# A linear attention and two MLPs on one core: the second pair of token chunks gets block products in its second layer, and work beside it goes to other steps

## The chip, the cores and the metric

The kernel runs on one core of one Trainium2 chip. The metric is the device time of one execution in microseconds, as the median of several runs. TensorE multiplies, VectorE (DVE in the profile) and ScalarE (ACT) convert, add and evict, GpSimd (POOL) and SyncE (SP) mostly issue DMAs. The clock that TensorE is granted has two levels, 1.2 and 2.4 GHz, and the profile gives it as a share of full speed.

## The reference

```python
# attention: q is normalised over the head's columns, k over the sequence
kv = np.einsum('bhsd,bhse->bhde', k_s, v)
x = np.einsum('bhsd,bhde->bhse', q_s, kv)      # 8 x 8 x 576 x 64 -> 4608 tokens x 512
# first MLP: 512 -> 2048 -> 512
h = x @ w_in
x = np.maximum(0.01 * h, h) @ w_out
# second MLP (MLP2): 512 -> 3 x 768 -> 512
h = np.maximum(np.maximum(x @ w1, x @ w2), x @ w3)
out = h @ w_out
```

Everything must come out with the accuracy of float32. The inputs come as 64-bit words; the kernel converts the weights itself.

## The kernel before

**Tiling.** The 4608 tokens are nine chunks of 512. Each operand of a matmul is split into a high and a low half in fp32r, and a product is three matmuls (high x high, high x low, low x high) of 128 x 128 by 128 x 512.

**First stage.** Chunks 0 to 2 go through the first MLP one by one (lines 1139 to 1196), m = 0 to 15 over blocks of 128 hidden columns, while attention for the next chunks and the conversion of the weights run beside them.

**Pairs.** Chunks 3 to 8 go through it as three pairs, `APAIRS` (line 30). Two chunks side by side are a 2 x 2 block matrix, and the first layer multiplies it by seven block products instead of eight (Strassen's scheme in Winograd's form, names a11, a12, s2, s1, s3, a22, s4). `InnerUnit` t = 0 to 7 does two m each: 7 products of 6 matmuls. The second layer of the first two pairs is plain: `out_a` (line 1210) multiplies the split halves of g (`split_g`, line 819) by weights `outw`, over 16 m for the left side beside the first layer and 16 m for the right side behind it; each side has 4 x 16 x 3 = 192 matmuls. The third pair goes through `inner_and_outer` (line 1758): its first layer writes quarters of the hidden matrix (`OuterPair.quarter`), and its second layer is seven block products behind it, 28 `TERMS` (name, q) of 12 matmuls. `build` makes the split operands `opO` three terms ahead, `load` fetches the weights `sumw` (each serves two terms), `finish` and `send` add and store the results. From term 18 `operands` builds what MLP2 needs first.

**MLP2** then takes five `PAIRS` in units u = 0 to 8 of seven block products, and for the first four pairs a `last_layer` (line 1516) of 21 terms with weights `lastw`. The first-MLP results of chunks 0 and 1 are partial sums in DRAM. `join` (line 938) adds them with accumulating DMAs on POOL's queue; `JOIN_AT` says in which pair's last layer.

**Order.** Work beside the main line is a set of generators: `background(step)` starts those whose step has come and advances each by one `yield`. Steps 0 to 47 are the first stage, 48 to 79, 80 to 111 and 112 to 143 the three pairs, in a plain pair three for each t and then one for every two m. `plan_units` gives attention its steps, `ahead_units` (line 948) the rest: `stage_a` and `sums_a` (sums of first-layer weights), `sums_out` (sums of second-layer weights, into `stream_sums`), `ahead_unit` (conversion, sums and split of MLP2's weights, into `stream`) and `ahead_out` (into `stream_last`). A planner orders what is ready on each engine; `pin` keeps an instruction in program order. So DMAs that depend on nothing late can run well ahead of their step.

**Room.** The pool `wp` has 17 buffers of 8 KB a partition, tag `w`, shared by weights, operands, quarters and rooms of the work beside; `xp` has two each of `xhi` and `xlo`, for attention results (`side`) and the rooms of the first weight units; `gp` has g, ghi, glo and st. PSUM has four banks `acc` and four `ps`.

Of the kernel before, what the change touches and what calls it, by code (L numbers as in the profile page):

```python
# [18 lines left out]
P = 128  # L19
N = 512  # L20
# [64 lines left out]
def tile_kernel(ctx: ExitStack, tc: tile.TileContext, q, k, v, wa, wb, out):  # L85
# [70 lines left out]
    newest = {}  # L156
    posted = []
# [87 lines left out]
    def to_stream(u, t, part):  # L245

        i = place(part, u)
        pin(nc.gpsimd.dma_start(stream[:, i], t))
        if i < 3:
            pin(nc.gpsimd.dma_start(stream[:, CYCLE + i], t))  # L250

# [94 lines left out]
    def ahead_out(t):  # L346
# [28 lines left out]
        for i, z in enumerate((more, room)):  # L375
            z = z.rearrange("p (h b n) -> p b h n", h=2, n=H)
            for b in range(4):
                pin(nc.gpsimd.dma_start(stream_last[:, 4 * i + b, t], z[:, b]))

    wos = {}  # L380

    def load_wo(t):

        w = wos[t] = wp.tile([P, 2, 2, N], F32R, tag="w", name="wo")
        for i, part in enumerate(("a11", "a12", "a21", "a22")):
            m, f = i % 2, i // 2
            to = w[:, :, m, f * H : f * H + H]
            pin(nc.sync.dma_start(to.bitcast(F32), stream_last[:, PARTS.index(part), t]))
# [471 lines left out]
    def stage_a(m):  # L860

        w = tiles[m].bitcast(F32)
        nc.sync.dma_start(stream_out[:, m], w[:, :, 1])
        i = m // 2 * len(AUSES)
        quarters = w[:, :, 0].rearrange("p h (b n) -> p b h n", n=H)
        for b in range(2):
            if m % 2 == 0:
                nc.sync.dma_start(stream_in[:, i + AUSES.index(("a11", "a12")[b])], quarters[:, b])
            elif b == 1:
                nc.sync.dma_start(stream_in[:, i + AUSES.index("a22")], quarters[:, b])  # L870
        yield

    def sums_a(t):
# [13 lines left out]
        for h, z in enumerate((hi, lo)):  # L887
            for at, n in ((0, 1), (1, 1), (2, 2)):
                to = i + AUSES.index(PARTS[4 + at])
                nc.sync.dma_start(stream_in[:, to : to + n, h], z[:, at : at + n])  # L890

    def sums_out(t):
# [12 lines left out]
        for h, z in enumerate((hi, lo)):  # L905
            nc.sync.dma_start(stream_sums[:, :, t // 4, h, t % 4], z)

# [7 lines left out]
    def plan_units(c):  # L915

        early = c < EARLY
        for hp in range(NP):
# [19 lines left out]
    def join(c):  # L938
# [169 lines left out]
    def load_in(g):  # L1108

        w = wp.tile([P, 4, 2, H], F32R, tag="w", name="group")  # L1110
        at = 4 * g % (len(AUSES) * MB_OUT)
        tc.keep_in_program_order(nc.sync.dma_start(w.bitcast(F32), stream_in[:, at : at + 4]))
# [7 lines left out]
    def load_out(n):  # L1120

        w = wp.tile([P, 2, 2, N], F32R, tag="w", name="outw")
        t = n % MB_OUT
        tc.keep_in_program_order(nc.sync.dma_start(w.bitcast(F32), stream_out[:, 2 * t : 2 * t + 2]))
        outs[n] = w

    def out_w(n):
# [3 lines left out]
        while len(outs) <= min(ahead, 2 * MB_OUT * (len(APAIRS) - 1) - 1):  # L1131
# [127 lines left out]
    def load_group(g):  # L1259
# [12 lines left out]
        for a, e in runs:  # L1272
            if a < e:
                ins = nc.sync.dma_start(w[:, a:e].bitcast(F32), stream[:, at + a : at + e])
# [46 lines left out]
    class Unit:  # L1321
# [14 lines left out]
        def snap(self, bank):  # L1336
            t = bp[0].tile([P, N], F32, tag="snap", name="snap", bufs=5)[:, : self.n]
            nc.scalar.activation(t, bank[:, : self.n], AF.Copy)  # L1338
            return t

        def out(self, i, bank, snap=None):

            bank = bank[:, : self.n]
            if self.j == 0:
                if self.layer is not None:
                    g = self.layer.quarter(i % 2 * 2 + i // 2, self.t)
                else:
                    tag, bufs = (("g", 2), ("ghi", 2), ("glo", 2), ("st", 4))[i]
                    g = gp.tile([P, N], F32, tag=tag, name=f"best{i}", bufs=bufs)[:, : self.n]
# [49 lines left out]
    class LastLayer:  # L1399
# [14 lines left out]
        def build(self, upto):  # L1414

            while len(self.made) < min(upto, len(LAST_TERMS)):
# [8 lines left out]
                tags = (("ghi", "glo"), ("ghi", "glo"), ("g", "g"), ("st", "st"), ("st", "st"))[k % 5]  # L1425
                hi, lo = (
                    gp.tile([P, N], F32R, tag=tag, name="opL", bufs=4 if tag == "st" else 2) for tag in tags
                )
# [6 lines left out]
        def load(self, upto):  # L1435

            while len(self.loaded) < min(upto, len(OUT_ORDER)):
# [3 lines left out]
                else:  # L1441
                    w = wp.tile([P, 4, 2, H], F32R, tag="w", name="lastw")[:, : MB // 2]
                pin(nc.sync.dma_start(w.bitcast(F32), stream_last[:, PARTS.index(name)]))
# [207 lines left out]
    class OuterPair:  # L1651
# [8 lines left out]
        def pair_of(self, x, q):  # L1660

            key = (x % 2, q)
            if key not in self.rooms:
                if q < 2 and x % 2 == 0:
# [28 lines left out]
        def load(self, upto):  # L1693

            for k in range(len(self.loaded), min(upto, 2 * len(OUT_ORDER))):
# [3 lines left out]
                if name in OUT_SUMS:  # L1699
                    pin(nc.sync.dma_start(f, stream_sums[:, OUT_SUMS.index(name), half]))  # L1700
                else:
                    odd, right = {"a11": (0, 0), "a12": (1, 0), "a22": (1, 1)}[name]
                    z = slice(MA // 2 * half + odd, MA // 2 * (half + 1), 2)
                    for h in range(2):
# [53 lines left out]
    def inner_and_outer(i, ops, fills):  # L1758
# [16 lines left out]
        for k, (name, q) in enumerate(TERMS):  # L1775
# [24 lines left out]
            if k == 18:  # L1800
                building = operands(quarters_b(sides), nxt, operand, fixed=True) if last else a_operands(i + 1, nxt)
            if k >= 18:
# [14 lines left out]
    for i in range(len(APAIRS)):  # L1817
        ops, nxt, building = begun_a, {}, iter(())
        last = i == len(APAIRS) - 1
        if last:  # L1820
# [8 lines left out]
            break  # L1829
# [59 lines left out]
        fills = [lambda f=f, i=i, pairs=pairs: out_a(i, 1, MA // 2 - 1, f, pairs) for f in range(KDM)]  # L1889
    for p in range(len(PAIRS)):  # L1890
# [3 lines left out]
        for u in range(NU):  # L1894
# [7 lines left out]
            iteration(Unit(p, u, ops, best, layer), *fill)  # L1902
            if not last and u in (3, 6):
# [89 lines left out]
```

## Time and profile before

| | us |
|---|---|
| median of 3 runs (lowest to highest) | 1378.44 (1372.72 to 1379.41) |
| profiled execution, own time | 1376.07 |
| its span, first to last instruction | 1374.3 |
| TensorE busy | 1347.8 |
| VectorE busy | 1007.1 |
| ScalarE busy | 710.9 |

The granted clock is full in all 40 slices of the page. Durations of matmuls overlap, so a rate is read from how long a run of them took. In the stages named below, the second pair's first layer begins at 473 us, interleaved with the end of the first pair, its second layer goes on until 693.7, the third pair's second layer runs from 761.9 to 848.4, and MLP2 follows.

### The profile page before, as it was taken

Reading aid. Unit: us, or ns where it says so; the run is one execution under the profiler, and the core shown is the slowest. Engines: PE = TensorE matmul, PEld = TensorE weight load, DVE = VectorE, ACT = ScalarE, POOL = GpSimd, SP = SyncE. Lnnn points to the kernel's source line nnn. Section 1 sums busy time; section 2 is a strip of 40 time slices with the busy share of each in tenths; the row PEclk is TensorE's granted clock in tenths of the full one; section 3 lists DMA queues with packets and bytes.
Section 4 is the critical chain, followed back from the end, with each engine's and each line's share of the span. In section 5 each row is a group of like instructions: output and inputs, shape, how many; then the busy total and the mean of one; then the engine's idle time right before and its main releaser. Section 6 shows DMA issues by size and latency. Waiting matters only on the chain.

```text
span 1374.3 us, 18904 instructions
## 1 busy us (share of the span) xinstructions
PE 1347.8 (98%) x6638; PEld 1107.5 (81%) x6638; DVE 1007.1 (73%) x1747; ACT 710.9 (52%) x1452; POOL 164.6 (12%) x251
## 2 busy tenths in 40 slices
PE   6999999999999999999999999999999999999998
PEld 5788877888788788888788888887788888888897
DVE  9988968864887797855958889767558657755743
ACT  6755857753776665744556554334225324423422
POOL 2001202200112120210313121211000000000000
PEclk9999999999999999999999999999999999999999
DMA  8698865535999967979678898999875584676684
GB/s 313 247 320 318 321 245 171 185 109 222 354 336 358 395 238 281 356 252 384 238 271 292 317 340 313 421 303 309 282 284 170 168 360 142 207 279 221 209 262 174
DMA packets 129502, 376.81 MB, mean 274 GB/s; under 512 B 12800, under 2 KB 68352, under 8 KB 105600
## 3 DMA queue, kind: packets, MB, share of 16 engines
q1 hardware_dynamic: 109936, 304.56, 61.1%
q0 software_dynamic: 18752, 66.72, 14.9%
q10 hardware_dynamic: 720, 4.33, 0.8%
q8 instruction: 53, 0.87, 0.2%
q14 instruction: 41, 0.34, 0.1%
HBM read 285.90 MB, written 96.99 MB: 279 GB/s over the span
## 4 chain that ended last, share of the span: by engine, by line
PE 89%; DVE 4%; DMA 3%; ACT 2%; issue 1%; SPq 0%; DVEq 0%; ACTq 0%
PE ps L1099 44%; PE acc L802 21%; PE ps L802 9%; PE acc L1456 6%; PE acc L1721 5%; PE ps L1456 1%; PE ps L628 1%; PE ps L496 1%; DMA lastw<-stream_last 1%; DMA outw<-stream_out 1%; PE ps L1721 1%; DMA spare<-in_q_dram 1%; DMA sumw<-stream_out 1%; DVE glo L826 0%; DVE opA L1060 0%
## 5 line engine op out<-in xcount | busy, mean ns | idle before, releaser
L1099 PE MATMUL ps<-op,group 128*128 128x512 f32 (+1 forms) x1890 | 395.7, 368 | 3.2 <-ACT snap L1338 3.2
L1099 PEld LDWEIGHTS ps<-op,group 128*128 128x128 f32 x1890 | 331.0, 188 | 65.5 <-ACT snap L1338 5.6
L1099 PE MATMUL ps<-opA,group 128*128 128x512 f32 x1008 | 241.5, 391 | 0.0
L1099 PEld LDWEIGHTS ps<-opA,group 128*128 128x128 f32 x1008 | 188.4, 188 | 39.8 <-ACT snap L1231 0.4
L1338 ACT ACTIVATE snap<-ps 128x512 f32<-128x512 f32 (+1 forms) x135 | 70.5, 552 | 196.4 <-PE ps L1099 191.8
L802 PE MATMUL acc<-ghi,outw 128*128 128x512 f32 x512 | 165.9, 392 | 1.5 <-ACT ghi L825 1.1
L802 PE MATMUL acc<-ghi,w 128*128 128x512 f32 x384 | 128.0, 394 | 1.7 <-ACT ghi L825 1.7
L802 PE MATMUL ps<-xhi,w 128*128 128x512 f32 x384 | 126.4, 393 | 1.1 <-ACT g L1151 0.7
L802 PEld LDWEIGHTS acc<-ghi,outw 128*128 128x128 f32 x512 | 95.4, 188 | 22.6 <-ACT ghi L825 2.5
L1358 DVE TENSOR_TENSOR snap<-snap,ps 128x512 f32<-128x512 f32 (+1 forms) x90 | 56.6, 632 | 77.5 <-ACT snap L1338 66.4
L1456 PE MATMUL acc<-opL,lastw 128*128 128x512 f32 x432 | 102.6, 394 | 1.8 <-DMA lastw<-stream_last 1.8
L802 PE MATMUL acc<-glo,outw 128*128 128x512 f32 x256 | 100.4, 393 | 1.3 <-DVE glo L826 1.1
L1456 PEld LDWEIGHTS acc<-opL,lastw 128*128 128x128 f32 x432 | 81.9, 190 | 19.9 <-ACT snap L1338 2.2
L1429 ACT ACTIVATE opL<-room 128x512 fp32r<-128x512 f32 x84 | 51.8, 629 | 73.6 <-DVE room L1360 38.4
L802 PEld LDWEIGHTS acc<-ghi,w 128*128 128x128 f32 x384 | 71.9, 188 | 18.0 <-ACT ghi L825 2.3
L802 PEld LDWEIGHTS ps<-xhi,w 128*128 128x128 f32 x384 | 72.0, 188 | 17.7 <-ACT g L1151 1.1
L826 DVE TENSOR_TENSOR glo<-g,ghi 128x512 fp32r<-128x512 f32 x80 | 54.8, 687 | 40.4 <-ACT ghi L825 40.2
L802 PE MATMUL acc<-glo,w 128*128 128x512 f32 x192 | 75.4, 393 | 0.0
L802 PE MATMUL ps<-xlo,w 128*128 128x512 f32 x192 | 74.9, 390 | 0.0
L1430 DVE TENSOR_TENSOR opL<-room,opL 128x512 fp32r<-128x512 f32 x84 | 56.6, 683 | 17.4 <-ACT opL L1429 16.6
L1721 PE MATMUL acc<-opO,sumw 128*128 128x512 f32 x288 | 66.6, 389 | 0.7 <-DMA sumw<-stream_out 0.7
L1721 PEld LDWEIGHTS acc<-opO,sumw 128*128 128x128 f32 x288 | 54.0, 188 | 12.3 <-DMA sumw<-stream_out 1.1
(220 smaller groups left out, 2094.5 us busy)
## 6 DMA issues: line engine op xcount, KB each, us to landing
group<-stream SPq DMA_DIRECT2D x78, 1024.0 KB, 9.0
group<-stream_in SPq DMA_DIRECT2D x42, 1024.0 KB, 7.3
outw<-stream_out SPq DMA_DIRECT2D x32, 1024.0 KB, 8.8
lastw<-stream_last SPq DMA_DIRECT2D x28, 768.0 KB, 4.7
stream<-room POOLq DMA_DIRECT2D x66, 256.0 KB, 4.1
raw<-in_wa_dram SPq DMA_DIRECT2D x16, 1024.0 KB, 7.1
room<-in_wb_dram POOLq DMA_DIRECT2D x24, 512.0 KB, 7.5
x<-st SPq DMA_DIRECT2D x40, 256.0 KB, 3.1
```

What stands on the lines that cost most here:

```text
L496: ins = nc.tensor.matmul(acc[z, : D + 1], lhsT=ke[:, r, z], rhs=vt[:, r, h], start=r == 0, stop=r == RK - 1)
L628: nc.tensor.matmul(both(xps, c0, c1), lhsT=a, rhs=halves(y, c0, c1), start=i == 0, stop=i == 2)
L802: ins = nc.tensor.matmul(acc, lhsT=l, rhs=r, start=first and i == 0, stop=last and i == 2)
L826: nc.vector.tensor_tensor(lo[:, z], g[:, z], hi[:, z].bitcast(F32), op=ALU.subtract)
L1099: ins = nc.tensor.matmul(bank[:, : r.shape[1]], lhsT=l, rhs=r, start=fresh and first, stop=last, skip_group_check=not fresh)
L1338: nc.scalar.activation(t, bank[:, : self.n], AF.Copy)
L1358: nc.vector.tensor_tensor(snap, snap, bank, op=ALU.add)
L1429: nc.scalar.activation(hi, z, AF.Copy)
L1430: nc.vector.tensor_tensor(lo, z, hi.bitcast(F32), op=ALU.subtract)
L1456: nc.tensor.matmul(banks[f], lhsT=l, rhs=r, start=fresh and first, stop=final, skip_group_check=not fresh)
L1721: nc.tensor.matmul(banks[f], lhsT=l, rhs=r, start=fresh and first, stop=final, skip_group_check=not fresh)
```

## The change

The second pair goes through `inner_and_outer` too (`PLAIN_OUT = 1` says how many pairs stay plain). Its quarters lie in buffers `w`, and those of x even and q = 3 in two buffers of a new tile `both` in `gp`, which holds ghi and glo side by side. The operands for the next pair are begun at term `NEXT_AT` = 20 in a pair that isn't the last. The steps of `sums_out` (`SO`), `ahead_unit` (`UA`), `ahead_out` (`AO`), `sums_a` (`SA`) and of attention (`LATER`) become tables with other numbers, and a weight unit is done in one go (`alone`) from u = 6 on, formerly from step 101 on. The joins are advanced at named units of MLP2, and before each adding DMA an ACT copy out of the newest `snap` and a small DMA of that copy stand in POOL's queue. Asserts (`need`) tell that what a load reads was written earlier in the program.

```diff
+NEXT_AT = 20
+PLAIN_OUT = 1
+SO = (45, 49, 51, 67, 68, 80, 81, 83)
+UA = (71, 77, 88, 98, 102, 106, 111, 114, 114)
+AO = (126, 131, 144)
+SA = (32, 34, 39, 44, 48, 53, 56, 60)
+LATER = ((0, 0), (43, 2.5), (71, 2.5))
+ALONE = 6
-JOIN_AT = (2, 1)
+JOIN_AT = ((2, 1), (2, 3), (2, 5), (2, 7), (1, 1), (1, 3), (1, 5))
...
-        hi = gp.tile([P, N], F32R, tag="ghi", name="ghi")
-        lo = gp.tile([P, N], F32R, tag="glo", name="glo")
+        both = gp.tile([P, 2, N], F32R, tag="both", name="ghl")
+        hi, lo = both[:, 0], both[:, 1]
...
-                start, lag = CONV * MA + 2 * MA * (i - 1) - (0, 3, 8)[i] + 2.5 * (4 * at + hp), 3
+                start, lag = LATER[i][0] + LATER[i][1] * (4 * at + hp), 3
...
-        for turn in mine[1:]:
+        for i, turn in enumerate(mine[1:]):
+            at = 4 * c + i
+            nc.scalar.activation(column[:, 0, at : at + 1], newest["snap"][:, 0:1], AF.Copy)
+            pin(nc.gpsimd.dma_start(column[:, 1, at : at + 1], column[:, 0, at : at + 1]))
             for z in (slice(0, 2), slice(2, 4)):
                 pin(nc.gpsimd.dma_start(joined[c][:, z], x2[turn][:, z], accum_op=ALU.add))
             yield
-            yield
...
-            yield (29, 34, 39, 44, 48, 52, 56, 60)[t], sums_a(t)
-        for t, at in enumerate((49, 50, 51, 73, 81, 82, 83, 84)):
-        for u, at in enumerate((68, 78, 88, 98, 103, 107, 112, 115, 119)):
-            yield at, ahead_unit(u, at > 100)
-        for t, at in enumerate((127, 135, 143)):
+            yield SA[t], sums_a(t)
+        for t, at in enumerate(SO):
+        for u, at in enumerate(UA):
+            yield at, ahead_unit(u, u >= ALONE)
+        for t, at in enumerate(AO):
...
-        live.extend(join(n) for n, p in enumerate(JOIN_AT) if p == layer.p)
...
         def pair_of(self, x, q):
             key = (x % 2, q)
+            if self.i < len(APAIRS) - 1 and key == (0, MA // 4 - 1):
+                if (x, q) not in self.rooms:
+                    self.rooms[x, q] = gp.tile([P, 2, N], F32, tag="both", name="quarter")
+                return self.rooms[x, q]
...
-            if k == 18:
+            if k == (18 if last else NEXT_AT):
                 building = operands(quarters_b(sides), nxt, operand, fixed=True) if last else a_operands(i + 1, nxt)
...
-            (ops, fills) = inner_and_outer(i, ops, fills)
+        if i >= PLAIN_OUT:
+            begun_a, fills = inner_and_outer(i, ops, fills)
+            ops = begun_a
...
+    joins = join(1), join(0)
...
+            if (p, u) in JOIN_AT:
+                next(joins[JOIN_AT.index((p, u)) < 4], None)
```

## Rows read from the trace of the kernel before

**Rows 1.** The page: busy us (share) x instructions; chain's shares by engine.
```profile
PE 1347.8 (98%) x6638; PEld 1107.5 (81%) x6638; DVE 1007.1 (73%) x1747; ACT 710.9 (52%) x1452; POOL 164.6 (12%) x251
PE 89%; DVE 4%; DMA 3%; ACT 2%; issue 1%; SPq 0%; DVEq 0%; ACTq 0%
```

**Rows 2.** Timeline of TensorE: start, length, line, tiles, shape, how many in a row.
```profile
345.05 4.24 PE L1099 MATMUL ps<-opA,group 128*128 128x512 f32 x18
...
776.50 11.04 PE L1721 MATMUL ps<-opO,sumw 128*128 128x512 f32 x48
```

**Rows 3.** Instructions of line 802: count, ns min/median/max, first and last start.
```profile
L802 PE MATMUL acc<-ghi,outw x512: 387/389/504, 339.3 to 693.7; 128*128 128x512 f32 x171
...
L802 PE MATMUL acc<-glo,outw x256: 387/389/505, 339.5 to 693.5; 128*128 128x512 f32 x128
```

**Rows 4.** Waits of TensorE, 530 to 694: us in total, times, longest.
```profile
PE acc L802 <- DVE glo L826: 1.1, 2, 0.6
PE acc L802 <- ACT ghi L825: 0.5, 1, 0.5
```

**Rows 5.** Waits of TensorE in the third pair, 694 to 850.
```profile
PE acc L1721 <- DMA sumw<-stream_out: 0.7, 1, 0.7
```

**Rows 6.** Timeline of TensorE in MLP2's first last layer.
```profile
960.34 5.96 PE L1456 MATMUL acc<-opL,lastw 128*128 128x512 f32 x18 [1.82 <-DMA lastw<-stream_last]
```

**Rows 7.** The stretch behind that wait: busy by engine, clock, DMA share, GB/s.
```profile
960.30:963.90 3.60, 3.56 (x9) 2.83 (x10) 0.17 (x1) 0.00 (x0) 0.00 (x0) 0.53 1.07 330
```

**Rows 8.** DMA, 925 to 962: POOL's queue (packets, MB, share); issues, us to landing.
```profile
q0 software_dynamic: 1004, 3.65, 51.8%
...
x<-x POOLq DMA_DIRECT2D x6, 512.0 KB, 9.5
lastw<-stream_last SPq DMA_DIRECT2D x3, 768.0 KB, 15.7
```

**Rows 9.** Stages: us, then busy PE, PEld, DVE, ACT, POOL; clock, DMA share, GB/s.
```profile
530.30:693.70 163.40, 161.56 (x728) 132.06 (x727) 117.75 (x198) 93.92 (x187) 31.89 (x45) 1.00 0.81 298
693.70:761.90 68.20, 68.20 (x302) 56.50 (x301) 45.72 (x68) 39.76 (x68) 19.17 (x28) 1.00 0.83 304
761.90:848.40 86.50, 85.81 (x379) 70.75 (x378) 80.43 (x97) 47.87 (x65) 11.70 (x18) 1.00 0.90 333
...
1081.00:1156.00 75.00, 74.31 (x328) 61.22 (x327) 42.89 (x66) 21.06 (x38) 0.00 (x0) 1.00 0.77 266
```

**Rows 10.** VectorE by line, 512 to 694 and 770 to 850: count | busy us, mean ns.
```profile
L826 DVE TENSOR_TENSOR glo<-right,ghi 128x512 fp32r<-128x512 f32 x19 | 12.9, 684 | 7.0 <-ACT ghi L825 6.9
...
L295 DVE TENSOR_TENSOR room<-room 128x512 fp32r<-128x512 f32 x15 | 9.9, 682 | 2.6 <-ACT room L294 2.6
L1060 DVE TENSOR_TENSOR opA<-side,opA 128x1024 fp32r<-128x1024 f32 x7 | 8.4, 1220 | 0.3 <-ACT opA L1059 0.3
L320 DVE TENSOR_TENSOR room<-room 128x1024 f32<-128x1024 f32 x5 | 6.1, 1221 | 0.1
...
L255 DVE TENSOR_TENSOR room<-room 128x256 f32<-128x256 f32 x9 | 3.8, 417 | 0.0
...
L281 DVE TENSOR_SCALAR room<-room 128x1024 f32<-128x1024 f32 x4 | 2.8, 688 | 1.1 <-ACT room L280 1.1
...
L1687 DVE TENSOR_TENSOR opO<-quarter,opO 128x1024 fp32r<-128x1024 f32 x25 | 30.3, 1220 | 4.5 <-ACT opO L1686 4.2 <-DMA group<-stream 0.3
```

**Rows 11.** Timeline of ScalarE: the first eviction of chunk 7's attention.
```profile
519.47 0.60 ACT L772 ACTIVATE side<-ps 128x512 f32<-128x512 f32 x1 [3.90 <-DMA stream<-room]
```

**Rows 12.** Timeline of TensorE: the second pair's second unit begins.
```profile
519.09 0.96 PE L1099 MATMUL ps<-opA,group 128*128 128x512 f32 x3
```

**Rows 13.** SyncE's own waits, 500 to 600: us in total, times, longest.
```profile
SPq L906 <- ACT hi L263: 14.4, 2, 10.4
```

**Rows 14.** The page's 40 slices of 34 us: VectorE's busy tenths.
```profile
DVE  9988968864887797855958889767558657755743
```

**Rows 15.** DMA issues, 765 to 850: KB each, us to landing.
```profile
sumw<-stream_sums SPq DMA_DIRECT2D x8, 1024.0 KB, 7.1
```

More of the change, by code (lines that the diff above doesn't have):

```diff
@@ L156, in tile_kernel, with need @@
     newest = {}
+    written = set()
+    def need(*keys):
+        assert written.issuperset(keys), [key for key in keys if key not in written]
     posted = []
@@ L378, in ahead_out @@
                 pin(nc.gpsimd.dma_start(stream_last[:, 4 * i + b, t], z[:, b]))
+                written.add(("last", 4 * i + b, t))
     wos = {}
@@ L387, in load_wo @@
             to = w[:, :, m, f * H : f * H + H]
+            need(("last", PARTS.index(part), t))
             pin(nc.sync.dma_start(to.bitcast(F32), stream_last[:, PARTS.index(part), t]))
@@ L863, in stage_a @@
         nc.sync.dma_start(stream_out[:, m], w[:, :, 1])
+        written.add(("out", m))
         i = m // 2 * len(AUSES)
@@ L868, in stage_a @@
                 nc.sync.dma_start(stream_in[:, i + AUSES.index(("a11", "a12")[b])], quarters[:, b])
+                written.add(("in", i + AUSES.index(("a11", "a12")[b])))
             elif b == 1:
                 nc.sync.dma_start(stream_in[:, i + AUSES.index("a22")], quarters[:, b])
+                written.add(("in", i + AUSES.index("a22")))
         yield
@@ L890, in sums_a @@
                 nc.sync.dma_start(stream_in[:, to : to + n, h], z[:, at : at + n])
+                written.update(("in", to + k) for k in range(n) if h == 1)
     def sums_out(t):
@@ L906, in sums_out @@
             nc.sync.dma_start(stream_sums[:, :, t // 4, h, t % 4], z)
+        written.add(("sums", t))
     def load_a(m):
@@ L1111, in load_in @@
         at = 4 * g % (len(AUSES) * MB_OUT)
+        need(*(("in", at + k) for k in range(4)))
         tc.keep_in_program_order(nc.sync.dma_start(w.bitcast(F32), stream_in[:, at : at + 4]))
@@ L1123, in load_out @@
         t = n % MB_OUT
+        need(("out", 2 * t), ("out", 2 * t + 1))
         tc.keep_in_program_order(nc.sync.dma_start(w.bitcast(F32), stream_out[:, 2 * t : 2 * t + 2]))
@@ L1130, in out_w @@
             ahead = max(ahead, min(n + AHEAD_OUT, n // (2 * MB_OUT) * 2 * MB_OUT + 2 * MB_OUT + 1))
-        while len(outs) <= min(ahead, 2 * MB_OUT * (len(APAIRS) - 1) - 1):
+        while len(outs) <= min(ahead, 2 * MB_OUT * PLAIN_OUT - 1):
             load_out(len(outs))
@@ L1273, in load_group @@
             if a < e:
+                need(*(("b", at + k) for k in range(a, e)))
                 ins = nc.sync.dma_start(w[:, a:e].bitcast(F32), stream[:, at + a : at + e])
@@ L1338, in snap @@
             nc.scalar.activation(t, bank[:, : self.n], AF.Copy)
+            newest["snap"] = t
             return t
@@ L1347, in out @@
                 else:
-                    tag, bufs = (("g", 2), ("ghi", 2), ("glo", 2), ("st", 4))[i]
-                    g = gp.tile([P, N], F32, tag=tag, name=f"best{i}", bufs=bufs)[:, : self.n]
+                    if i == 2:
+                        t = gp.tile([P, 2, N], F32, tag="both", name="best12")[:, :, : self.n]
+                        self.best[1], self.best[2] = t[:, 0], t[:, 1]
+                    elif i != 1:
+                        tag, bufs = (("g", 2), None, None, ("st", 4))[i]
+                        self.best[i] = gp.tile([P, N], F32, tag=tag, name=f"best{i}", bufs=bufs)[:, : self.n]
+                    g = self.best[i]
                 self.best[i] = g
@@ L1424, in build @@
                 z = {"a11": b11, "a12": b21, "s2": b11, "s3": b12, "s1": b12, "a22": b21, "s4": b22}[name]
[L1425 to L1428, printed above, removed]
+                tag = ("both", "both", "g", "st", "st")[k % 5]
+                if tag == "both":
+                    o = gp.tile([P, 2, N], F32R, tag=tag, name="opL")
+                    hi, lo = o[:, 0], o[:, 1]
+                else:
+                    hi, lo = (
+                        gp.tile([P, N], F32R, tag=tag, name="opL", bufs=4 if tag == "st" else 2) for _ in range(2)
+                    )
                 nc.scalar.activation(hi, z, AF.Copy)
@@ L1442, in load @@
                     w = wp.tile([P, 4, 2, H], F32R, tag="w", name="lastw")[:, : MB // 2]
+                need(*(("last", PARTS.index(name), t) for t in range(MB // 2)))
                 pin(nc.sync.dma_start(w.bitcast(F32), stream_last[:, PARTS.index(name)]))
@@ L1699, in load @@
                 if name in OUT_SUMS:
+                    need(*(("sums", t) for t in range(MA // 4 * half, MA // 4 * (half + 1))))
                     pin(nc.sync.dma_start(f, stream_sums[:, OUT_SUMS.index(name), half]))
@@ L1703, in load @@
                     z = slice(MA // 2 * half + odd, MA // 2 * (half + 1), 2)
+                    need(*(("out", k) for k in range(z.start, z.stop, 2)))
                     for h in range(2):
@@ L1825, in tile_kernel @@
             tp = tp_ctx.enter_context(tc.tile_pool(name="tp", bufs=1))
[L1826 removed]
+        if i >= PLAIN_OUT:
+            begun_a, fills = inner_and_outer(i, ops, fills)
+            ops = begun_a
+        if last:
             tp_ctx.close()
             bp.append(ctx.enter_context(tc.tile_pool(name="bp", bufs=1)))
[L1829 removed]
+        if i >= PLAIN_OUT:
+            continue
         for t in range(MA // 2):
```

6 lines of the change are left out of this document (4 added, 2 removed).

## Prediction

> **What bounds the kernel now.** I read the page's busy times and its chain first. TensorE is busy 98% of the span and holds 89% of the chain that ended last [rows 1], so the time is the number of matmuls times the distance between two of them, plus the places where TensorE stands. The distance is not the 389 ns duration, because matmuls overlap: 18 in a row took 4.24 us, the last of them 0.39, so (4.24 - 0.39) / 17 = 0.227 us; 48 in the block products of the second layer give (11.04 - 0.39) / 47 = 0.227 as well [rows 2]. The second view is the waits of TensorE by stage. In the second pair's second layer it stood 1.1 + 0.5 us for the split halves of g [rows 4]; in the third pair, whose two layers already are block products, 0.7 us [rows 5]. The third view is the timeline where it stood longest after the start: 1.82 us for the last layer's weights, `lastw` [rows 6].
>
> **What the change removes.** (1) Matmuls. The two plain second layers have 512 + 256 matmuls on `outw` [rows 3], 384 for each pair. Seven block products are 28 terms of 2 x 2 x 3 = 12 matmuls, 336. The second pair saves 48 x 0.227 = 10.9 us, all of it on the chain. (2) The waits of that plain layer, 1.6 us [rows 4]: its halves are no longer split one m at a time. (3) The wait for `lastw`. The granted clock behind it was 0.53, which is the 1.2 GHz level, for 3.6 us [rows 7], so its 18 matmuls took 5.96 us where 17 x 0.227 + 0.39 = 4.25 would do: 1.82 + 1.7 = 3.5 us. While that load was under way the POOL queue kept the DMA engines 51.8% busy, with the accumulating copies of `join` (six issues in 37 us, landing in 9.5 us), and `lastw` needed 15.7 us to land [rows 8]. The code asks for these joins in the last layers of MLP2 pairs 1 and 2, but they depend on nothing late, so POOL ran them one pair ahead. The change puts an ACT copy of a fresh `snap` and a small DMA in front of each on POOL, in units of pairs 1 and 2. Behind the waiting DMA stand only the other joins: POOL's weight units are finished by then. Together 10.9 + 1.6 + 3.5 = 16.0 us.
>
> **What it adds.** (4) VectorE work in the second pair. Gone are 32 subtractions of 512 columns at 0.684 us, 21.9; new are 28 of 1024 columns at 1.22 for the operands, 16 more of that size for the sums of quarters and 6 adds of 0.68: 34.2 + 19.5 + 4.1 [rows 10]. That is 35.9 us more, in a stage that gets shorter. The nearest row is the third pair's second layer, where VectorE is busy 80.4 of 86.5 us and TensorE still did not wait for it [rows 5, 9]. It holds two conversions of MLP2 weights. The second pair's will hold about 2.4 (those begun at steps 98 and 102, part of 106, the tail of 88), each three operations of 0.69, three of 1.22, three of 0.68 and five of 0.42 = 9.9 us [rows 10], so some 84 us of VectorE work against (336 + 12) x 0.227 = 79 us of TensorE. Five too many. If all slides into the third pair's first layer, where VectorE is busy only 45.7 of 68.2 us, it costs 0; if TensorE pays the 5 and the 6.1 us that VectorE was idle there too, 11. An operand is asked for three terms, 3 x 2.72 = 8.2 us, ahead, so I take 2, near the lower end.
>
> (5) The hand-over into the second pair's first layer. Block products keep two PSUM banks of a unit alive into the next one, so with four banks an attention result that is not yet evicted stands in the way. Before, ACT stood 3.9 us on the first such eviction, until 519.5, for `stream<-room`, the room of the first weight unit, and TensorE did not notice [rows 11]: the second unit of products had only begun, at 519.1 [rows 12]. That weight unit now begins three steps later. A step is a third of a plain unit of 66 x 0.227 = 15 us, so the room can come free up to 15 us later, and the second unit's `a12`, which wants the bank some 1.4 us behind 519.1, can wait 14. Bounds 0 and 14; the weight unit waited for VectorE, not for its step, and VectorE loses one sum of weights in this stretch and has attention work behind it sooner, so I take 1.5.
>
> (6) SyncE's queue. Three sums of weights (steps 80, 81, 83) put their stores there, and such stores waited up to 10.4 us for ACT [rows 13] with the next `group` loads queued behind them. Plain units use a group in 15 / 1.75 = 8.6 us, block products in 24 x 0.227 = 5.4, two ahead: 10.9 us of cover against the store's wait and the load's own time. Bounds 0 and 6; I take 1, since the third pair shows no wait for a group [rows 5].
>
> (7) The joins in their new places: each is 2 issues among block products whose DMA share is 0.77 [rows 9]. At the rate of rows 8 they fill the engines there. Bounds 0 and 3.5, the price they had; 0.5, because groups are fetched three ahead there and no `lastw` is due. The seven ACT copies and small DMAs run beside matmuls.
>
> Costed at nothing: the merged tile of ghi and glo (same bytes, same last reader), and the earlier attention and sums of weights, which go to the end of the first stage, where the VectorE digits drop to 6 and 4 [rows 14]. If that cover fails, each sum delays TensorE by at most its own VectorE work, 1.22 + 4 x 0.42 = 2.9 us. That the weights' sums are early enough is clear: the last begins at step 83, the first load that needs them comes in the second layer, after step 96.
>
> **Sum.** -16.0 + 2 + 1.5 + 1 + 0.5 = -11.0 us. The profiled execution took 1376.07 us (span 1374.3, 1.8 around it), so 1365.1; it lay 2.4 under the median of the three runs, 1378.44, and that median less 11.0 is 1367.4. I predict **1367**.
>
> **The rivals.** *Nothing new stops TensorE* (the third pair's 0.7 us is all that a block layer costs): 1378.4 - 16.0 = 1362. For it: rows 5. Against it: the third pair has no attention and no sums of weights.
>
> *VectorE becomes the bound of the second pair.* It costs 11 instead of 2: 1367.4 + 9 = 1376. For it: 80.4 of 86.5 us busy in the same layer, and four more to come [rows 9]; against it: TensorE did not wait there, and there is room behind. The Trainium skill, page "Perfetto Trace Analysis", section "Identifying the Most-Contended Engine", judges VectorE by its occupancy and TensorE not by matmul busy time but by that of LDWEIGHTS, and tells to optimise the most occupied engine first. By that rule VectorE, 93% against 70.8 / 86.5 = 82% for weight loads, is the engine to relieve in this layer, and the change loads it: 1376. The trace so far does not bear it out: in that layer TensorE's one wait was for a DMA.
>
> *The weights of the second layer come late: slower.* Its place is the pool of 17 buffers `w`. In the second pair's second layer seven hold quarters (the third pair has two in another pool), two hold groups fetched for the third pair, and from term 10 two hold a weight unit. Six are left for four operands and for `sumw`, and then a load goes out only when the one before the last is used up. A load serves two terms, 5.45 us, and lands in 7.1 [rows 15], plus 0.3 for the issue: about 1.95 us late, nine times, 17.6 us, and up to twice that when the clock falls behind each wait as in rows 7. 1367.4 + 17.6 = 1385, up to 1402; I put it at 1388. It decides as soon as one `sumw` less is held ahead through most of the layer. Against it: in the third pair the raw sides and two `ahead_out` take as many buffers, and only the first load was waited for [rows 5].
>
> *The joins are not held back* (the change doesn't do what it says), or their new places cost what the old one did: the 3.5 us stay, 1367.4 + 3.5 = 1371.
>
> **How the numbers follow.** Chances: forecast 0.42, nothing new 0.17, VectorE 0.15, joins 0.10, late weights 0.16. The runs shown spread 1372.7 to 1379.4, so half a per cent, 6.9 us, is about what a measurement can tell from no change: faster means under 1371.5, slower over 1385.3. Faster takes the forecast but for its tail (0.36), all of "nothing new", two fifths of VectorE and half of the joins: 0.64. Slower takes most of late weights: 0.13. Same: 0.23. The range reaches from the lowest run less the full gain, 1372.7 - 16 = 1357, rounded to 1358, up over the VectorE case to 1382; late weights lie outside.
>
> **What would show it.** Right: 336 matmuls for the second pair's second layer, and 48 fewer than the 6638 in all; no idle TensorE before `lastw` of MLP2's first pair, joins at two DMAs a unit in pairs 1 and 2, and a full clock throughout. Step 4 is wrong if TensorE waits for `opO` there by ACT or VectorE for over 4 us; step 5 if it stands before the second unit's a12; step 6 if it stands for `group`; the slower rival shows as repeated waits for `sumw` with a clock under 1. Wrong altogether: a pair that loses more than 16 us in such waits.

## The result, and the profile after

The changed kernel took 1385.1 us (1383.2 to 1389.2, six runs) against 1377.3 of the kernel before beside it: a ratio of 1.0065 [1.0046, 1.0084], slower by 6 to 12 us where 11 less were forecast. Its profiled execution took 1383.19 us with a span of 1381.4, 7.1 over the span before. The page's busy times and the shares of its chain, against rows 1:

```profile
PE 1340.1 (97%) x6590; PEld 1098.3 (80%) x6590; DVE 1040.8 (75%) x1765; ACT 722.9 (52%) x1455; POOL 167.0 (12%) x258
PE 81%; DVE 8%; DMA 5%; issue 2%; ACT 2%; POOL 1%; SPq 0%; ACTq 0%; DVEq 0%; POOLq 0%
```

TensorE has the 48 matmuls less, and the chain that ended last has 8 points less of TensorE, 4 more of VectorE, 2 more of DMA [rows 1]. Where the 7.1 us came from is read by stages: the second pair (from the time at which its products began before), the third pair's first layer, its second, and all of MLP2. Columns as in rows 9. Before:

```profile
473.00:683.00 210.00, 208.16 (x961) 169.50 (x961) 162.01 (x268) 120.51 (x237) 40.48 (x58) 1.00 0.80 291
683.00:761.90 78.90, 78.90 (x349) 65.34 (x348) 50.76 (x78) 45.52 (x78) 21.04 (x30) 1.00 0.79 287
761.90:848.40 86.50, 85.81 (x379) 70.75 (x378) 80.43 (x97) 47.87 (x65) 11.70 (x18) 1.00 0.90 333
848.40:1374.30 525.90, 516.63 (x2438) 432.14 (x2436) 336.54 (x563) 182.43 (x341) 23.28 (x30) 1.00 0.74 253
```

The same stages after:

```profile
473.00:682.40 209.40, 199.94 (x900) 162.03 (x901) 169.32 (x246) 123.86 (x216) 32.16 (x47) 0.99 0.80 284
682.40:774.90 92.50, 82.78 (x349) 65.98 (x348) 71.14 (x103) 50.80 (x83) 30.80 (x44) 0.98 0.86 299
774.90:863.10 88.20, 88.20 (x390) 73.02 (x390) 82.40 (x102) 47.99 (x65) 13.96 (x20) 1.00 0.90 314
863.10:1381.40 518.30, 511.83 (x2426) 428.96 (x2424) 333.05 (x557) 182.86 (x346) 21.86 (x29) 1.00 0.75 254
```

The second pair is 0.6 us shorter instead of 10.9: some 10 us are lost in it. The third pair's first layer, whose 349 matmuls did not change, went from 78.9 to 92.5: 13.6 us lost. MLP2 gave 7.6, partly by matmuls that lie a stage earlier (12 here, 11 more in the stage before). What TensorE waited for (us in total, times, longest), in the second pair (471 to 682) and then in the third pair's first layer (682 to 775):

```profile
PE acc L819 <- DVE ghl L843: 2.9, 2, 1.5
PE ps L1123 <- DMA group<-stream_in: 2.6, 1, 2.6
PE ps L645 <- DVE snap L1661: 1.7, 2, 0.9
PE ps L1123 <- ACT snap L1257: 1.3, 1, 1.3
PE ps L513 <- DVE snap L1661: 0.8, 1, 0.8
PE acc L1764 <- ACT snap L1257: 0.8, 1, 0.8
PE ps L1123 <- ACT side L789: 0.6, 1, 0.6
...
PE ps L1123 <- DMA group<-stream_in: 5.9, 4, 4.4
PE ps L1123 <- DVE opA L1084: 1.9, 1, 1.9
PE ps L1123 <- ACT snap L1257: 1.7, 1, 1.7
```

The longest wait, 4.4 us for a `group`, can be followed one step further back. SyncE's queue issues these loads, and each takes a buffer of the pool `w`. In the third pair's first layer that queue itself stood for buffers which POOL's stores of a weight unit's room (`stream<-room`) had yet to return, up to 10.4 us at a time, all between 725 and 746. Behind these waits a load went out at 739.9 and landed at 745.9, and TensorE went on at 746.0. SyncE's waits of this kind, first in the kernel before (683 to 761.9), then in the change (682 to 775):

```profile
SPq L1112 <- DMA stream<-room: 37.5, 6, 14.3
SPq L1137 <- DMA stream<-room: 17.2, 4, 10.4
```

SyncE stood there before as well, and longer in total, yet TensorE waited for no load: the wait alone is not the price, but a load that goes out too late behind it.

No single wait of TensorE is as long as the loss, and the clock adds to them: the longest, 4.37 us until 746, is followed by a stretch with a granted clock of 0.69 on the mean of 5.5 us, so partly at the lower level of 1.2 GHz.

```profile
746.03 29.08 PE L1123 MATMUL ps<-opA,group 128*128 128x512 f32 x120 [4.37 <-DMA group<-stream_in]
...
746.00:751.50 5.50, 5.47 (x17) 4.45 (x18) 2.43 (x6) 1.37 (x3) 2.15 (x3) 0.69 0.83 331
```

Below, the **excess** of a stage is the sum over successive TensorE starts that lie clearly further apart than a pipelined pair (over 0.285 us for 512 columns) of what they take above 0.227 us: waits and half clock together. It is read from one execution of each kernel, and executions of the same work can differ in a stage by several us (last section). Before: 4.5 us in the second pair, 0.0 and 1.0 in the third pair's two layers, 8.9 in MLP2. After: 14.0, 13.4, 0.0 and 4.3.

### The profile page after: what moved, and what is told of

Same layout as the page of the kernel before. It is cut to its first block, busy times and chain, and to the rows that moved or that the text cites. A ratio compares the mean times of both kernels' runs of the same rounds, so it can differ in the third digit from the quotient of the medians.

```text
span 1381.4 us, 18884 instructions
## 1 busy us (share of the span) xinstructions
PE 1340.1 (97%) x6590; PEld 1098.3 (80%) x6590; DVE 1040.8 (75%) x1765; ACT 722.9 (52%) x1455; POOL 167.0 (12%) x258
## 4 chain that ended last, share of the span: by engine, by line
PE 81%; DVE 8%; DMA 5%; issue 2%; ACT 2%; POOL 1%; SPq 0%; ACTq 0%; DVEq 0%; POOLq 0%
PE ps L1123 39%; PE acc L819 13%; PE ps L819 9%; PE acc L1764 8%; PE acc L1494 7%; DMA room<-in_wb_dram 1%; PE ps L513 1%; DMA stream<-room 1%; PE ps L1494 1%; PE ps L645 1%; DMA group<-stream_in 1%; DMA outw<-stream_out 1%; PE ps L1764 1%; DVE room L310 1%; DVE opO L1728 1%
## 5 line engine op out<-in xcount | busy, mean ns | idle before, releaser
L1123 PE MATMUL ps<-opA,group 128*128 128x512 f32 x1008 | 244.8, 396 | 14.2 <-DMA group<-stream_in 8.5
L819 PE MATMUL acc<-ghl,w 128*128 128x512 f32 x576 | 143.3, 393 | 1.3 <-ACT ghl L842 1.3
L1764 PE MATMUL acc<-opO,sumw 128*128 128x512 f32 x576 | 132.8, 389 | 0.8 <-ACT snap L1257 0.8
L1764 PEld LDWEIGHTS acc<-opO,sumw 128*128 128x128 f32 x576 | 108.0, 188 | 23.6 <-ACT snap L1257 1.2
L819 PEld LDWEIGHTS acc<-ghl,w 128*128 128x128 f32 x576 | 107.1, 188 | 24.7 <-ACT ghl L842 1.8
L819 PE MATMUL acc<-ghl,outw 128*128 128x512 f32 x384 | 96.1, 395 | 4.3 <-DVE ghl L843 2.9
L819 PEld LDWEIGHTS acc<-ghl,outw 128*128 128x128 f32 x384 | 70.6, 188 | 21.3 <-DVE ghl L843 4.2
L1727 ACT ACTIVATE opO<-quarter 128x1024 fp32r<-128x1024 f32 x56 | 58.5, 1056 | 45.0 <-PE acc L1764 27.8
L1728 DVE TENSOR_TENSOR opO<-quarter,opO 128x1024 fp32r<-128x1024 f32 x56 | 67.8, 1217 | 7.5 <-ACT opO L1727 7.3
L843 DVE TENSOR_TENSOR ghl<-g,ghl 128x512 fp32r<-128x512 f32 x64 | 43.9, 687 | 26.9 <-ACT ghl L842 26.7
```

The lines of the kernel that those rows point to most:

```text
L819: ins = nc.tensor.matmul(acc, lhsT=l, rhs=r, start=first and i == 0, stop=last and i == 2)
L843: nc.vector.tensor_tensor(lo[:, z], g[:, z], hi[:, z].bitcast(F32), op=ALU.subtract)
L1123: ins = nc.tensor.matmul(bank[:, : r.shape[1]], lhsT=l, rhs=r, start=fresh and first, stop=last, skip_group_check=not fresh)
L1727: nc.scalar.activation(o[:, 0], t, AF.Copy)
L1728: nc.vector.tensor_tensor(o[:, 1], t, o[:, 0].bitcast(F32), op=ALU.subtract)
L1764: nc.tensor.matmul(banks[f], lhsT=l, rhs=r, start=fresh and first, stop=final, skip_group_check=not fresh)
```

## The experiments

**The joins alone.** The kernel before, with only the joins tied to units:

```diff
-JOIN_AT = (2, 1)
+JOIN_AT = ((2, 1), (2, 3), (2, 5), (2, 7), (1, 1), (1, 3), (1, 5))
+            nc.scalar.activation(column[:, 0, at : at + 1], newest["snap"][:, 0:1], AF.Copy)
+            pin(nc.gpsimd.dma_start(column[:, 1, at : at + 1], column[:, 0, at : at + 1]))
```

> The kernel before, with nothing of the change but the joins tied to units of MLP2. Theory of the prediction: the wait for lastw at 960 us and the half clock behind it go, 3.5 us, so some 1373.8 against 1377.3. Rival (the copies cost the same wherever they stand, or aren't held back): 1377 within 1.

Measured: 1373.0 us, ratio 0.9958 [0.9943, 0.9973]. The excess of MLP2 fell from 8.9 to 5.2, that of the pairs did not move, and the wait for `lastw` is gone. This is faster than both kernels, and the rest of the change therefore costs some 12 us over it.

**Which part of the rest.** Four kernels from the changed one. The first has a plain second pair under the new steps (`PLAIN_OUT = 2`); the second has all steps of before (the lists SO, UA, AO, SA, LATER and ALONE), the third only those of the weight units, the fourth only those of sums and attention.

```diff
-PLAIN_OUT = 1
+PLAIN_OUT = 2
```
```diff
-UA = (71, 77, 88, 98, 102, 106, 111, 114, 114)
-AO = (126, 131, 144)
-ALONE = 6
+UA = (68, 78, 88, 98, 103, 107, 112, 115, 119)
+AO = (127, 135, 143)
+ALONE = 4
```

> The changed kernel with PLAIN_OUT = 2: the second pair's second layer is plain again, all other edits stay (steps of sums, weight units and attention, merged tile, joins). If the loss comes with the block products of the second pair (VectorE, banks or buffers), this gives what the joins give, 1373 to 1375. If the moved steps cost by themselves, it stays over 1380.

> The changed kernel with every step as before the change: sums, weight units, their alone rule, ahead_out and attention; block products in the second pair, joins and the merged tile stay. Theory now (the moved steps cost, the block products gain): 1373 of the joins alone less most of the 10.9 us of matmuls, 1363 to 1369. Rival (block products in the second pair cost what they save under any steps): 1373 or more. Second rival (only with the moved steps does the second pair come through): over 1385.

> The changed kernel with the steps of the weight units alone (UA, the alone rule, AO) as before; sums and attention at the new steps. If the units' steps make the third pair wait, this takes back the waits of TensorE between 696 and 750 us, 12 us with the half clock: 1371 to 1375. If attention and sums do it, 1383 to 1387.

> The changed kernel with attention and sums (LATER, SO, SA) at the steps before, weight units at the new ones: the complement of the run with old units. If attention and sums make the loss, 1371 to 1375; if the units do, 1383 to 1387. Neither alone: both over 1380.

Measured: 1393.3 (1.0105 [1.0088, 1.0123]), 1400.9 (1.0175 [1.0151, 1.0199]), 1380.9 (1.0043 [1.0019, 1.0066]) and 1404.8 (1.0216 [1.0186, 1.0245]). So the block products gain 8 us under the new steps (1393 to 1385) and lose 28 under the old ones (1373 to 1401); steps and products belong together. Of the new steps, those of sums and attention are worth 20 us; those of the weight units seem to cost 4, but the two intervals overlap. No kernel takes back the merged tile of ghi and glo by itself: it is in all four of these and not in the joins alone. In the fourth kernel TensorE waited 10.9 us for `ghl` and 3.2 for `kvlo` between 460 and 860, against 2.9 and none in the change: attention and halves of g that come too late.

**Two suspects that were wrong.** PSUM banks: the attention results of chunks 7 and 8 into the other four banks. VectorE: five operations of each conversion of MLP2 weights left out, 0.69 + 0.69 + 1.22 + 0.69 + 1.22 = 4.5 us of it each.

```diff
-        acc = psum()
+        acc = ps_acc.tile([P, N], F32, tag="acc", name="acc") if (b, hp) == (7, 3) else psum()
-        xps = psum()
+        xps = ps_acc.tile([P, N], F32, tag="acc", name="acc") if (c, hp) > (7, 0) else psum()
```
```diff
-        pin(nc.vector.tensor_scalar(af, af, MOST_HIGH, LEAST_HIGH, op0=ALU.min, op1=ALU.max))
...
-        nc.vector.scalar_tensor_tensor(bf, low, 2.0**-52, bf, op0=ALU.mult, op1=ALU.mult)
```

> The changed kernel, but the attention results of chunks 7 and 8 that fall into the second pair's first layer (queries from the second on, the last key) go to the acc banks of PSUM, which are idle there, and not to the four ps banks. Theory of banks: the three waits of attention matmuls for a snap (0.85 us each) and those behind the first eviction (0.6 and 1.3 us) go, 2.5 to 4.5 us: 1381 to 1383. Rival (these waits only take the place of later ones for VectorE or DMA): within 1.5 of 1385.

> The changed kernel with five of the VectorE operations of every MLP2 weight conversion left out (three of 0.69 and two of 1.22 us, 4.5 us a unit, over nine units and three ahead_out; the converted weights are not the reference's). Rooms, DMAs, ScalarE work and steps stay. If VectorE's load of the second pair is the root and late rooms are its consequence, the waits of TensorE in the second pair and in the third pair's first layer (excess 14.0 and 13.4 us) fall by more than half: 1366 to 1374. If the number of buffers is the root by itself, units hold them for their DMAs all the same: 1380 or more.

Measured: 1385.3 (1.0058 [1.0037, 1.0078]) and 1386.1 (1.0074 [1.0045, 1.0103]). Neither moved the time. With 48 us less of VectorE on the page (993.2), ScalarE's longest single wait between 682 and 790, 10.3 us, was for a quarter of the third pair whose buffer a store had to return (line numbers are 5 lower there; this profiled execution was the longest of its seven, 1397.1 us, so the length of the wait is not typical):

```profile
ACT quarter L1248 <- DMA stream<-room: 14.9, 2, 10.3
```

**The order, and the units.** First, products of the second pair's first layer not pinned in program order; then the change with weight units 6 to 8 left out, whose parts of `stream` are copied in DRAM from those of units 0 to 2; then both.

```diff
-            multiply(bank, in_w(at), self.ops[name], fresh, pinned=True)
+            multiply(bank, in_w(at), self.ops[name], fresh, pinned=self.i == len(APAIRS) - 1)
```
```diff
+        if u >= 6:
...
+                pin(nc.gpsimd.dma_start(stream[:, i], stream[:, k]))
...
+            return
```

> The changed kernel, but the first-layer products of the second pair are free to be ordered among the end of the first pair, as they were in the plain form, and not kept in program order. If the fill-in of those products covered VectorE's delays before, the waits for ghl at 472 and 513 us and the bank waits go: 1379 to 1383. If not: 1385 within 2, or slower where the free order costs banks.

> The changed kernel with the last three weight units of MLP2 left out (in their place DRAM copies of other units' parts, so these weights are not the reference's). Their six rooms in w and their work on ScalarE and VectorE are gone from the third pair's first layer; block products in the second pair stay. If those rooms starve the group loads and hold the quarters of the third pair, its excess of 13.4 us falls under 3: 1371 to 1376. If the group loads are late for the DMA rate or SyncE's queue, over 1381.

> Change with the second pair's first-layer products not pinned and weight units 6 to 8 left out (their parts copied in DRAM from earlier units, so those products use the wrong weights). Two losses that add: 1376 less 6 to 10, that is 1366 to 1370. If one loss hides the other (the same wait moved about): 1375 to 1377.

Measured: 1379.1 (1.0016 [0.9998, 1.0034]); 1376.1 (0.9989 [0.9973, 1.0004]); 1365.1 (0.9923 [0.9903, 0.9942]). The first took the excess of the second pair from 14.0 to 3.5, the second that of the third pair's first layer from 13.4 to 2.6, and together they bring 20 us against 6 + 9 alone. The losses are two. Four pairs of kernels on record differ in the pin alone, two of them further below, and unpinned is faster in each: by 6 us (1385.1 to 1379.1), 11 (1376.1 to 1365.1), 10 (1389.3 to 1379.0) and 9 (1386.2 to 1376.9). Unpinned alone, the third pair takes a part back: its two layers have 19.0 us of excess then, against 13.4 in the change. The timeline of TensorE where the first pair ends shows what the pin does, in the change, then unpinned, then in the kernel before:

```profile
504.29 6.02 PE L819 MATMUL acc<-ghl,outw 128*128 128x512 f32 x24
510.46 1.19 PE L819 MATMUL acc<-ghl,outw 128*128 128x512 f32 x4 [0.15 <-ACT ghl L842]
513.12 8.23 PE L819 MATMUL acc<-ghl,outw 128*128 128x512 f32 x35 [1.46 <-DVE ghl L843]
```
```profile
505.13 1.65 PE L1123 MATMUL ps<-opA,group 128*128 128x512 f32 x6
506.62 1.09 PE L819 MATMUL acc<-ghl,outw 128*128 128x512 f32 x4
507.56 1.58 PE L1123 MATMUL ps<-opA,group 128*128 128x512 f32 x6
508.97 4.70 PE L819 MATMUL acc<-ghl,outw 128*128 128x512 f32 x20
513.51 1.52 PE L1123 MATMUL ps<-opA,group 128*128 128x512 f32 x6
```
```profile
473.39 1.19 PE L802 MATMUL acc<-ghi,outw 128*128 128x512 f32 x4
474.42 1.53 PE L1099 MATMUL ps<-opA,group 128*128 128x512 f32 x6
```

Pinned, the first pair's tail is alone on TensorE and stands for its split halves; unpinned, the next pair's products lie in the gaps, as they did in the kernel before from 473 on. This stretch holds only 1.6 of the 10.9 us that TensorE waited in the second pair. The waits for a group, for attention's banks and for ScalarE's first eviction are gone as well when unpinned, and 3.6 us are left (471 to 682); how the free order removes each of them was not followed.

```profile
PE ps L1123 <- ACT snap L1257: 2.0, 3, 0.7
PE acc L819 <- DVE ghl L843: 1.6, 1, 1.6
```

In the last kernel, without units 6 to 8, TensorE's waits in the third pair's first layer (673 to 757) are only the 2.1 us for its first operands (line numbers are 11 higher there):

```profile
PE ps L1134 <- DVE opA L1095: 1.9, 1, 1.9
PE ps L1134 <- ACT opA L1094: 0.2, 1, 0.2
```

**The rooms of these units.** In the change their rooms are buffers of `w`, as groups and quarters are. Beside the group loads in SyncE's queue, ScalarE's timeline shows what they hold up: a quarter and a room, each waiting until a store of POOL's queue has landed.

```profile
722.23 0.63 ACT L1253 ACTIVATE quarter<-snap 128x512 f32<-128x512 f32 x1 [2.53 <-DMA stream<-room]
...
729.03 1.16 ACT L295 ACTIVATE room<-room 128x1024 f32<-128x1024 f32 x1 [2.87 <-DMA stream<-room]
```

Three kernels put rooms into the pool of `x`: of units 6 to 8; of 6 and 7; of 6 and 7 with products unpinned.

```diff
-        first, second = a_room(u >= WIDE), a_room(u >= WIDE)
+        first, second = (a_room(u in (4, 5, 8)) for _ in range(2))
```

> The changed kernel, but weight units 6 to 8 take their two rooms in xp (xhi, xlo), which is empty in the third pair, and not in the pool w. Theory of buffers: in the third pair's first layer six rooms in w keep back the group loads, which cost TensorE 5.9 us of idle there and about as much at half clock; with rooms in xp these waits go, 8 to 12 us, so 1374 to 1377. Rival (VectorE has too much to do and everything after it is late, whatever the buffers): within 2 us of 1385.

> The changed kernel, but of the last three weight units only unit 8 takes its rooms in w; 6 and 7 take theirs in xp, which has room for two units and is empty in the third pair. All work stays, so this tells the rooms from the work: if the rooms in w made the third pair's 13.4 us of excess, it falls under 4, and the time to 1374 to 1378, as in the run without these units; if their work on ScalarE and VectorE made it, 1383 to 1387. (The run with all three in xp could not tell, since the third unit had to wait for the first one's room with ScalarE behind it.)

> The two edits together: units 6 and 7 take their rooms in xp, and the second pair's first-layer products are free in their order. If the two losses are separate (second pair 10 us, third pair 10 to 12), they add up: 1385 - 10 - 11 = 1364 to 1369, faster than the kernel before and than the joins alone (1373). If freeing the order only moves the stall into the third pair, 1376 or more.

Measured: 1396.9 (1.0130 [1.0106, 1.0154]), 1389.3 (1.0101 [1.0070, 1.0132]) and 1379.0 (1.0014 [0.9996, 1.0032]): no gain. The waits for `group` went, but with 6 and 7 in `x` a quarter's buffer came from a weight unit (by the code unit 8, the only late one left in `w`), ScalarE stood 10.0 us for it (690 to 790), and TensorE 6.06 for ScalarE:

```profile
ACT quarter L1253 <- DMA stream<-room: 10.0, 1, 10.0
...
769.36 2.93 PE L1123 MATMUL ps<-opA,group 128*128 128x512 f32 x6 [6.06 <-ACT snap L1257]
```

**The last unit later.** All three units in rooms of `x`, the last at step 122 (unpinned, then pinned), 125 or 128; and at 128 with the last `ahead_out` taking its conversion three steps later behind its loads.

```diff
-UA = (71, 77, 88, 98, 102, 106, 111, 114, 114)
+UA = (71, 77, 88, 98, 102, 106, 111, 114, 122)
-        first, second = a_room(u >= WIDE), a_room(u >= WIDE)
+        first, second = (a_room(u in (4, 5)) for _ in range(2))
```
```diff
-        for _ in range(5):
+        for _ in range(5 if t < 2 else 8):
```

> Change with the second pair's first-layer products not pinned, units 6, 7 and 8 in rooms of x (none in w), and unit 8 taken at step 122 instead of 114, when the store of unit 6's room has long landed. Theory, rooms: what the late units cost in the third pair's first layer is ScalarE standing behind a room or quarter that a store has yet to give back; with no room in w and a later last unit that wait goes, the stage's excess falls from about 13 us to 5 or less, and the time is 1366 to 1370. Rival, the units' own work presses the stage, wherever their rooms are: 1377 to 1380, as with two rooms and no pin (1379.0).

> The same rooms and the later last unit, products pinned as in the change. Rooms theory with losses that add: 1375 to 1378, which is 8 to 10 us below the change. If the pin's loss comes only from units that slip: 1366 to 1370, as without pins. Rival, the units' own work: 1385 to 1389, no better than the change.

> Second pair's products not pinned, units 6 to 8 in rooms of x, the last unit at step 125: between 122 (1376.9, third pair's two layers 15.1 us of excess, nothing behind) and 128 (1382.8, 7.7 us there, 13.7 behind). If the late load at 864 comes from the last unit being behind the second MLP's first unit in POOL's order (at 128 it is, at 125 it is not): no wait at 864, and 1370 to 1376. If it is only the time of the stores: a part of the wait, 1378 to 1381.

> As the first kernel of this set, unit 8 at step 128. Rooms theory: within 2 us of step 122, as the room is free at both. If the last unit then comes too late for its first product, a wait of TensorE for its stream shows at the start of the third pair's second half and the time is above the first kernel's by its length.

> As the kernel with the last unit at step 128, and the last weight unit of the second MLP waits three steps more between its loads and its first conversion. Theory, in-order ScalarE stood behind that load: the wait of 11.4 us at 864 and the half clock behind it go, 1368 to 1372. Rival, the units' work moves its press on to the next place: 1377 to 1383.

Measured: 1376.9 (1.0007 [0.9987, 1.0027]), 1386.2 (1.0070 [1.0046, 1.0093]), 1377.2 (1.0009 [0.9994, 1.0023]), 1382.8 (1.0051 [1.0034, 1.0067]) and 1380.0 (1.0024 [1.0007, 1.0041]). The theory of rooms alone, 1366 to 1372, fell. The excess by stage says why (second pair | third pair's first layer | its second | MLP2, us):

```
step 122          7.7 |  8.2 |  6.9 |  4.3
step 125          3.8 |  4.1 | 12.7 |  4.3
step 128          5.0 |  2.7 |  5.0 | 18.0
128, later conv. 12.5 |  2.7 |  5.1 | 11.6
```

The loss behind the second pair goes where the unit goes. ScalarE's waits for a transfer, in the kernels with step 122 (620 to 760) and then 125, 128 and 128 with the later conversion (760 to 900):

```profile
ACT room L295 <- DMA room<-in_wb_dram: 7.0, 2, 4.2
```
```profile
ACT opO L1727 <- DMA stream_last<-room: 9.8, 1, 9.8
```
```profile
ACT room L295 <- DMA room<-in_wb_dram: 14.8, 1, 14.8
```
```profile
ACT room L295 <- DMA room<-in_wb_dram: 9.4, 1, 9.4
```

And what TensorE then waited, at steps 125 and 128:

```profile
832.87 0.80 PE L1764 MATMUL acc<-opO,sumw 128*128 128x512 f32 x1 [5.44 <-ACT opO L1727]
```
```profile
875.43 24.90 PE L1123 MATMUL ps<-op,group 128*128 128x512 f32 x99 [11.38 <-ACT snap L1365]
```

The kind is the same in these two, and in the kernels with rooms in `x`: an instruction of ScalarE whose buffer or data a transfer of POOL's queue has yet to return or bring, and behind it, in the order of ScalarE's timeline, the operand or the eviction that TensorE waits for. In the change itself the longest wait came through SyncE's queue and its group loads. Of the kernels with block products in the second pair, only those without these units left the wait no next place. What stays open: leaving the units out takes away their rooms, their transfers and their work on ScalarE at once, so that the buffers are the cause is read from the waits and not separated by a run; which of the transfers is late first; and whether a step can be found for all of them that beats the joins alone.

## Why the prediction was wrong, step by step

- **Step 1**, the matmuls: right, 6590 of them, at the same distance.
- **Step 2**, the waits of the plain layer: near. One wait of 0.8 us is left in that layer, where there were 1.6.
- **Step 3**, `lastw`: right. The joins alone are worth 3.7 to 7.8 us by the interval, 3.5 less 0.5 were forecast with step 7, so a little too few. TensorE no longer waits there, and between 925 and 962, where `lastw` took 15.7 us to land [rows 8], POOL's queue moves nothing and it takes 4.4:

```profile
lastw<-stream_last SPq DMA_DIRECT2D x4, 768.0 KB, 4.4
```

- **Step 4**, VectorE: the work was sized well, 33.7 us more on the page against 35.9, and the 2 us for the layer itself were too many: VectorE is busy 72.6 of 80.4 us there (602 to 682.4), and TensorE waits for no `opO`. **The step failed in what it put behind the layer**: what slides into the third pair's first layer "costs 0" there. 20.4 us of VectorE's work did come into it, and VectorE is still busy only 71.1 of 92.5 us, yet the stage lost 13.6 us. It was judged by VectorE's idle time; what TensorE waited for there was `group` (5.9 us), its first operands (2.1) and ScalarE (1.7). Ahead of the longest of these waits SyncE's queue, and beside it ScalarE, stood for buffers of `w` that stores of weight units had yet to return. Without units 6 to 8 the stage's excess is 2.6 us.
- **Step 5**, the hand-over: the mechanism was there and its size about right. ScalarE stood 7.4 us for `stream<-room` instead of 3.9 [rows 11], and TensorE 0.6 + 1.3 behind it. With other banks the time was the same.
- **Step 6**, groups: forecast 1 us, measured 2.6 in the second pair and 5.9 in the third. The first is the forecast's mechanism: a store of sums stood 8.8 us for ScalarE in SyncE's queue, until 552.7, the group loads went out behind it, and TensorE stood until 562.3. The second is another one, in its longest wait buffers of `w` that stores had yet to return, which the step did not have.
- **Missing from the sum**: through `inner_and_outer` the second pair's first-layer products are pinned in program order, as the third pair's were. The forecast took no price for it; unpinning them takes 10.5 us from the second pair's excess (14.0 to 3.5) and 6 from the time, 9 to 11 in three other pairs of kernels. Nor did it have the 2.1 us for the third pair's first operands, which the kernel before did not wait for and which stay without units 6 to 8.
- **The rivals.** "Late weights" had the right pool, `w`, and the right sign, but the wrong place: `sumw` of the second layer was not waited for at all, the loads that came late were groups, a layer further on. That its 1388 lies near 1385.1 is luck. "VectorE becomes the bound" fell with the lighter conversions: 1386.1 us with 48 us less of VectorE, not less than 1385.1. In the second pair's second layer VectorE was busy 72.6 of 80.4 us against 65.5 for weight loads. The rule of the Trainium skill that this rival draws on ("Perfetto Trace Analysis", section "Identifying the Most-Contended Engine": relieve the most occupied engine first) would for this layer have sent one to VectorE, which gave nothing; the measurement decides against it here.

By excess the account closes to about 1 us: -10.9 for matmuls, -4.6 for MLP2, +9.5 in the second pair, +13.4 and -1.0 in the third and about +1.1 in the stages ahead make some +7.5, against 7.1 in the spans.

## What to carry to other kernels

When work is moved behind a busier stage, don't ask only whether the engine that computes it has time there; list the queues that will stand for its buffers and transfers (here SyncE's and ScalarE's), and what is queued behind that. When a stage is rewritten, see whether its instructions were free to fill in for the stage ahead and still are. And test the cheap part alone first: of the kernels here that do all of the work, the one with only the joins was the fastest (1373.0).

## What was not expected of the hardware

Executions of one kernel scatter by several us: 1372.5 to 1380.2 us (22 runs) for the kernel before, 1374.3 to 1385.2 (12) for the last unit at 128 with the later conversion, 1372.3 to 1383.7 (10) at step 122, 1372.6 to 1379.4 (10) without units 6 to 8. Some spread less, over fewer runs: 1371.9 to 1373.4 (4) for the joins alone, but also 1380.5 to 1383.2 (4) at step 128, where ScalarE had its longest wait for a load. So the runs don't tie the scatter to such waits.

In the two kernels with the last unit at 128, in which every engine runs the same instructions in the same order until 873 us, the wait of ScalarE for the same load of raw weights, near 635 us, was 1.23 and 6.59 us, and the excess of the second pair 5.0 and 12.5:

```profile
633.76 1.13 ACT L295 ACTIVATE room<-room 128x1024 f32<-128x1024 f32 x1 [1.23 <-DMA room<-in_wb_dram]
```
```profile
638.69 1.12 ACT L295 ACTIVATE room<-room 128x1024 f32<-128x1024 f32 x1 [6.59 <-DMA room<-in_wb_dram]
```

So one profiled execution can put several us into a stage that another does not, and excesses of single executions are to be read with that in mind. The two ran on different chips; whether that or chance made the difference was not tested.
